# Two attention and feed-forward layers on one core: a new start, and a table that moves single operations in the planner's order

## The chip, the cores and the metric

The kernel runs on one core of one Trainium2 chip. The time is device microseconds of one execution. The engines are named as in the profile: PE multiplies matrices (PEld is its weight load), DVE and ACT work on vectors, POOL is GpSimd, SP issues most of the DMA transfers, and ACT issues some as well.

## What is computed

The input x is 2048 tokens by 640 features in bf16. Two kinds of block alternate, A, B, A, B, with the same weights in both turns:

```python
x = x + _A_ref(_layernorm(x), wq, wk, wv, wo, beta)
x = x + _B_ref(_layernorm(x), w1, w2)
x = x + _A_ref(_layernorm(x), wq, wk, wv, wo, beta)
x = x + _B_ref(_layernorm(x), w1, w2)
```

Block A is attention with 32 heads of 20 features in four segments of 512 tokens. In each segment and head it takes a causal softmax attention within the segment and, with phi(t) = t + 1 for t > 0 and exp(t) otherwise, a read from a memory that the earlier segments wrote:

```python
p = softmax(qs @ ks^T * scale + mask);  a_dot = p @ vs
a_mem = (phi(qs) @ M) / (phi(qs) @ z + 1e-06)
o = sigmoid(beta) * a_mem + (1 - sigmoid(beta)) * a_dot
M = M + phi(ks)^T @ vs;  z = z + sum(phi(ks))
```

The result is multiplied by wo. Block B is max(x @ w1, 0) @ w2 with a hidden width of 1728.

## The kernel before

All weights and x stay on the chip. Work goes by segments of 512 tokens, each four tiles of 128 tokens. For one segment of block A, layer norm is computed token by token on DVE (`stats`: two BN_STATS per tile at L694 and an aggregate at L696), the power -1/2 on POOL (`chain`, L710), the scaling on DVE (L740). The result is transposed by a DMA (`turn`, L716) into `xnT` (for early segments into a part of `hT`). Products with wq, wk (to `stg`) and wv (to `v_aug`) run on PE as groups of five matmuls (`group`, L673). Their results leave PSUM by DVE or ACT (`evac`; L872 and L873 for q and k, L927 for v). q and k go through a scratch tensor in DRAM, and SP loads them back head by head into `pad` (`fill`, L1008), 20 features at the foot of each group of 32 partitions.

Scores (L1192) multiply four heads at a time, in five rounds for each pair of head groups, two rounds' halves together. ACT takes the exponential (L1254, 320 of them), POOL clears what lies behind the diagonal (L1266), and PE multiplies by v (L1286; for the first eight groups, L1325). DMA transposes turn the result back into tokens (`otk`), DVE divides (L1372 to L1380) and adds the memory read (L1072 on PE, L1084 to L1087 on DVE, L1399). The sum `o_sb` is transposed to `oT` (`turn_o`) and multiplied by wo. The memory write is L1129, with its update of `M_sb` and `BD` on DVE. Block B is `ffn` (L1490 and L1491 evict the hidden layer, L1512 adds to x).

A product can be issued in two forms. The full form is one matmul of 128 rows and 128 columns (L673). The quarter form is four matmuls of 128 rows and 32 columns each (L676), which stand on four quarters of the columns; the product with v (L1286) is always of this kind. Scores use 20 rows and 128 columns (the row form).

The order is not written by hand. Each part of the work is a Python generator, a stream, that yields operations; `Sched.run` holds a planned clock for every engine, and at each step takes, of all streams' next operations, the one with the smallest key: planned start plus an allowance, then priority, then segment. The result is a fixed list of instructions for each engine; every engine works its list in order and waits at semaphores. So a planned duration that is changed, or a key that is moved, can change the lists of all engines. PE's form (full or quarter) is chosen by the planner too, from the form that PE last used and from what is due soon.

The start has an order of its own. `loads` issues the transfers for the first four tiles of x (two on SP, two on ACT), then on SP the first columns of wk and wq (c below 2), their remaining columns, wv, and the second segment's x. `warm_pe` multiplies the identity 52 times (L650), which waits for POOL to make it. Tiles 0 and 1 take their statistics on DVE, each with its own POOL chain; tiles 2 and 3 take theirs on ACT (`first_ln_b`): both sums (L805), one mean (L808), both sums of squares (L812), then one chain for both. `first_tile` scales each tile (L752), transposes it on PE (L764) and copies it to `xnT` (L771, L773). `proj_first` then makes q and k for feature chunks c = 0 and 1 in two halves, two tiles (256 tokens) each, and for the other chunks whole. `first_heads` sends chunk 0 and a part of chunk 1 straight from `stg` to the first pads (L988; four transfers on SP, five on ACT). Beta, which every partition needs, is loaded on SP when the second segment's x has been issued (L627), and ACT takes its exponential (L630); the mask `maskg` is made on POOL (L614 to L622).

Of the kernel before, what the change touches and what calls it, by code (L numbers as in the profile page):

```python
# [10 lines left out]
D = 640  # L11
# [161 lines left out]
HOLDERS = 1  # L173
HOLD_TOL = {"pe": 220.0, "act": 150.0, "dve": 200.0, "pool": 0.0, "sp": 0.0}


class Sched:
# [120 lines left out]
    def run(self):  # L298
        while True:
# [24 lines left out]
            for prio, n, st, alts, op, late in heads:  # L324
# [9 lines left out]
                key = (round(start + late), 0.5 if op.urgent else prio, self.rank[id(st[1])], n)  # L334
# [94 lines left out]
def bass_interleave_layers__memory_aug_infini_attn__dense_activation_relu__prompt_kernel(  # L429
    nc, A_x, A_wq, A_wk, A_wv, A_wo, A_beta, B_x, B_w1, B_w2, out,  # L430
):
    with contextlib.ExitStack() as es:
# [13 lines left out]
        ident = sb("ident", [128, 128])  # L446
        warm = sb("warm", [128, 1], dt.float32)
        asum = sb("asum", [128, 4], dt.float32)
        beta_bc = sb("beta_bc", [128, H])
# [3 lines left out]
        stats6 = sb("stats6", [128, 12, 2, 6], dt.float32)  # L453
# [19 lines left out]
        om_sb = sb("om_sb", [128, NJ, D])  # L473
        rden = sb("rden", [128, 2, 2, NJ, 4, 1], dt.float32)
# [48 lines left out]
        def ld(e, name, nbytes, fn, waits=()):  # L523
            tk = yield dma(e, sem_("d_" + name), nbytes, fn, waits, lat=1550.0 if name[:2] == "x0" else 2000.0)
            S.set(name, tks=[tk])
# [7 lines left out]
        def loads():  # L533
# [58 lines left out]
        def consts():  # L592
            tw = yield dve(4, 1, lambda e: e.memset(warm[:], 0.0))
            yield act(4, lambda e: e.activation(warm[:], warm[:], ACT.Exp), [tw], psum=False)
            t0 = yield pool(150, lambda e: e.memset(ident[:], 0.0))
            t1 = yield pool(250, lambda e: e.affine_select(
                out=ident[:], in_=ident[:], compare_op=ALU.not_equal, fill=1.0, base=0,
# [28 lines left out]
            yield Need("x11")  # L626
# [3 lines left out]
            te = yield act(32, lambda e: e.activation(gt[:, 0, :], beta_bc[:], ACT.Exp), [tb], psum=False)  # L630
# [14 lines left out]

        def warm_pe():

            idt = yield Need("ident")
            yield Acq([X])
            tk = yield pe(4600.0, [(lambda e: e.matmul(  # L650
                ps[:, 0, 0:128], ident[:], ident[:], start=True, stop=True), k == 51) for k in range(52)], idt)
            X.release(tk)

# [37 lines left out]
        def stats(t, xt):  # L691
            tk = None
            for c2 in range(2):
                tk = yield dve(320, 1, lambda e, c2=c2: e.bn_stats(  # L694
                    stats6[:, t % 12, c2, :], x_sb[:, t, c2 * 320:(c2 + 1) * 320]), xt)
# [940 lines left out]
```

## Time and profile before

| | |
|---|---|
| time, median of 3 runs | 556.43 us (555.3 to 559.99) |
| span of the profiled execution | 553.7 us; the median lies 2.7 us above it |
| PE busy | 545.7 us (99%), 8,340 matmuls |
| DVE busy | 414.2 us (75%) |
| ACT busy | 408.7 us (74%) |
| POOL busy | 191.9 us (35%) |
| chain that ended last | 89% PE, 5% DVE, 2% DMA, 2% ACT |
| granted clock | 1.000 |

The profile's page is one execution. Its own time is known as its span, from the first to the last instruction; what lies around it in a timed run is taken as the difference to the median. Busy shares are means over the whole span, so the views by stretch and the timeline tell more: the timeline gives start and length in us of runs of equal instructions, with the idle time ahead of them and what ended it in brackets. A run of n equal matmuls is as long as n - 1 distances from start to start and one matmul from its start to its end (0.30 us for 320 elements, 0.38 us for 512), since matmuls overlap.

### The profile page before, as it was taken

The numbers are of one execution on the slowest core, as the hardware profiler recorded it, in microseconds if no ns is written. First come the engines' busy times: TensorE is split into PE (matmuls) and PEld (weight loads), VectorE is DVE, ScalarE is ACT, GpSimd is POOL, SyncE is SP. The second block draws the span as 40 slices with busy tenths as digits, with TensorE's granted clock in tenths as the row PEclk, the third lists the DMA queues.
The fourth block names the chain that finished last, engine by engine and source line by source line (L and its number), as shares of the span: only waits on it lengthen the run. The fifth ranks groups of instructions, "written<-read, shape, count | busy, mean of one in ns | idle before, by whom it ended". The sixth has DMA issues, their size and how long they took to land.

```text
span 553.7 us, 19086 instructions
## 1 busy us (share of the span) xinstructions
PE 545.7 (99%) x8340; PEld 308.3 (56%) x8340; DVE 414.2 (75%) x1059; ACT 408.7 (74%) x518; POOL 191.9 (35%) x302
## 2 busy tenths in 40 slices
PE   8999999999999999999999999999999999999998
PEld 7464554455564555646446555565456654657756
DVE  5967989897898988997687998669886886417202
ACT  5699889889877888687887887778874878651140
POOL 5245344343444334343433443034430433301000
DMA  8595999933854138466276332971439322342201
GB/s 271 134 232 158 227 186 211 239 72 45 191 112 91 32 58 199 79 93 92 60 188 107 60 69 21 207 147 22 67 48 223 92 36 54 69 81 28 74 2 51
DMA packets 130292, 61.32 MB, mean 111 GB/s; under 512 B 109090, under 2 KB 120098, under 8 KB 130210
## 3 DMA queue, kind: packets, MB, share of 16 engines
q1 hardware_dynamic: 129648, 59.58, 50.8%
q8 instruction: 65, 1.06, 0.8%
q10 hardware_dynamic: 562, 0.53, 0.3%
q14 instruction: 17, 0.14, 0.1%
HBM read 20.57 MB, written 12.85 MB: 60 GB/s over the span
## 4 chain that ended last, share of the span: by engine, by line
PE 89%; DVE 5%; DMA 2%; ACT 2%; POOL 0%; SPq 0%; issue 0%; ACTq 0%; POOLq 0%
PE ps L673 42%; PE ps L676 27%; PE ps L1192 8%; PE ps L1286 6%; ACT PT L1254 2%; PE ps L1325 1%; PE ps L1072 1%; PE ps L650 1%; DMA oT<-o_sb 1%; DMA otk<-otu 1%; PE ps L1466 1%; PE ps L1129 1%; DVE hT L1490 1%; DVE xn_tok L740 1%; DMA beta_bc<-in_A_beta_dram 1%; DVE o_sb L1380 1%
## 5 line engine op out<-in xcount | busy, mean ns | idle before, releaser
L1254 ACT ACTIVATE PT<-ps 128x1024 bf16<-128x1024 f32 x320 | 309.0, 1026 | 58.6 <-PE ps L1192 57.3
L1266 POOL TENSOR_SCALAR_AFFINE_SELECT PT<-PT 128x512 bf16<-128x512 bf16 x256 | 166.6, 669 | 266.8 <-ACT PT L1254 266.7
L673 PE MATMUL ps<-w_r,hT 128*128 128x320 bf16 x488 | 78.5, 300 | 0.0
L1512 DVE TENSOR_TENSOR x_sb<-x_sb,ps 128x320 bf16<-128x320 bf16 (+1 forms) x65 | 31.1, 479 | 48.1 <-PE ps L676 34.1
L676 PE MATMUL ps<-xnT,w_r 128*32 128x512 bf16 x1092 | 64.8, 379 | 0.1
L1192 PE MATMUL ps<-pad 20*128 20x512 bf16 (+3 forms) x1024 | 63.4, 301 | 1.2 <-ACT PT L1254 1.0
L673 PE MATMUL ps<-xnT,w_r 128*128 128x512 bf16 x247 | 60.9, 380 | 0.0
L673 PEld LDWEIGHTS ps<-w_r,hT 128*128 128x128 bf16 x488 | 45.6, 98 | 23.5 <-issue 6.4
L694 DVE BATCH_NORM_STATS2 stats<-x_sb 128x6 f32<-128x320 bf16 x124 | 56.0, 474 | 2.6 <-DMA x_sb<-in_A_x_dram 2.2
L676 PE MATMUL ps<-w_r,hT 128*32 128x320 bf16 (+1 forms) x1428 | 52.4, 294 | 0.0
L1192 PEld LDWEIGHTS ps<-pad 20*128 20x128 bf16 x1024 | 17.8, 92 | 52.2 <-ACT PT L1254 28.1
L1491 ACT ACTIVATE hT<-ps 128x512 bf16<-128x512 f32 x51 | 30.5, 598 | 20.5 <-PE ps L676 19.6
L676 PEld LDWEIGHTS ps<-w_r,hT 128*32 128x32 bf16 x1428 | 37.0, 97 | 10.2
L676 PEld LDWEIGHTS ps<-xnT,w_r 128*32 128x32 bf16 x1092 | 28.3, 97 | 24.6 <-issue 0.5
L1296 DVE CAST otu<-ps 128x512 bf16<-128x512 f32 x50 | 34.2, 684 | 8.7 <-PE ps L1286 8.2
L1490 DVE TENSOR_SCALAR hT<-ps 128x512 bf16<-128x512 f32 x53 | 36.1, 682 | 6.1 <-PE ps L673 4.6
L1408 DVE TENSOR_TENSOR x_sb<-x_sb,ps 128x320 bf16<-128x320 bf16 x64 | 29.6, 477 | 14.7 <-PE ps L676 7.3
L1286 PE MATMUL ps<-PT,v_aug 128*21 128x128 bf16 (+3 forms) x896 | 40.4, 301 | 0.0
L1037 ACT ACTIVATE stg<-stg 128x512 bf16<-128x512 bf16 x50 | 31.6, 635 | 8.5 <-DVE rtmp L1035 8.5
L673 PE MATMUL ps<-wo_r,oT 128*128 128x320 bf16 x234 | 37.0, 300 | 0.3 <-DMA oT<-o_sb 0.3
L710 POOL TENSOR_TENSOR rstd<-lnU,mhalf 128x2 f32<-128x2 f32 (+2 forms) x26 | 20.3, 780 | 47.5 <-DVE lnU L706 37.6
L673 PEld LDWEIGHTS ps<-xnT,w_r 128*128 128x128 bf16 x247 | 22.2, 97 | 25.3 <-issue 3.7
(109 smaller groups left out, 737.2 us busy)
## 6 DMA issues: line engine op xcount, KB each, us to landing
pad<-scr SPq DMA_DIRECT2D x124, 80.0 KB
scr<-stg SPq DMA_DIRECT2D x34, 256.0 KB, 2.9
out_dram<-x_sb SPq DMA_DIRECT2D x15, 160.0 KB, 2.2
w_r<-in_B_w_dram SPq DMA_DIRECT2D x10, 216.0 KB, 2.5
w_r<-in_B_w_dram SPq DMA_DIRECT2D x13, 160.0 KB, 3.0
x_sb<-in_A_x_dram SPq DMA_DIRECT2D x10, 160.0 KB, 3.4
scr<-w_r SPq DMA_DIRECT2D x5, 256.0 KB, 2.9
wv_r<-in_A_wv_dram SPq DMA_DIRECT2D x1, 800.0 KB, 8.8
```

The costliest lines, as they stand in the source:

```text
L673: return e.matmul(view(dst.ap, b), a, b, start=(k == 0), stop=(k == last))
L676: return e.matmul(view(dst.ap[rows], b), part, b, start=(k == 0), stop=(k == last))
L694: tk = yield dve(320, 1, lambda e, c2=c2: e.bn_stats(stats6[:, t % 12, c2, :], x_sb[:, t, c2 * 320:(c2 + 1) * 320]), xt)
L1037: te = yield act(512, lambda e, q=q: e.activation(q, q, ACT.Exp), [tr] + p, psum=False)
L1192: fns.append([(lambda e, z=z, j=j, hh=hh, N=N, o=o, sl=sl, q=hh % 2: e.matmul(slot.ap[:, q, o:o + N], sl.ap[32 * hh:32 * hh + DH, z, 0, 12 ...
L1254: tx = yield act(1024, lambda e, dst=dst, src=src: e.activation(dst, src, ACT.Exp, scale=SCALE), sc + pw)
L1266: tm = yield pool(600.0, lambda e, reg=reg: e.affine_select(out=reg, in_=reg, pattern=[[0, 4], [1, 128]], compare_op=ALU.is_ge, fill=0.0, ...
L1286: fns.append((lambda e, OD, j=j, hh=hh: e.matmul(OD.ap[32 * hh:32 * hh + DH + 1, 128 * j:L], VAUG[vx(a, s)][:, j, 4 * g + hh, :], pt.ap[:, ...
L1296: te = yield evac(L, 1, lambda e: e.tensor_copy(dst, OD.ap), lambda e: e.activation(dst, OD.ap, ACT.Copy), [tk] + OTU[0].tks)
L1490: th = yield evac(512, 1, lambda e: e.tensor_scalar(hT[:, dc, :], bk.ap[:, :], 0.0, None, ALU.max), lambda e: e.activation(hT[:, dc, :], b ...
L1491: lambda e: e.activation(hT[:, dc, :], bk.ap[:, :], ACT.Relu), [tk] + HT.tks)
L1512: ta = yield dve(n, 1, lambda e: e.tensor_tensor(x_sb[:, t, c0:c0 + n], x_sb[:, t, c0:c0 + n], bk.ap[:, 0:n], ALU.add), [tk], urgent=True)
```

## The change

- A table `SHIFT` is added to the key of the planner, by stream and segment: 86 entries from -3000 to 4300 ns. It moves where an operation is put, and adds none.
- Planned costs change: a pair of score rounds 233 instead of 221 ns, the power on POOL 520 or 700 instead of 740, the first x loads 1470 instead of 1550, and two DVE operations (`BD` and the last of `divide`) are planned with the port that they share with POOL.
- `warm_pe` uses a tile of ones, set by DVE, in the first PT buffer instead of the identity, and 41 matmuls instead of 52; five more stand behind tile 0's transposes. The identity lies in a part of `om_sb`. The first statistics tile has a place for each of the 16 tiles.
- Beta is loaded as one row of 64 bytes, third in ACT's queue, into a tile that is otherwise zero, and a matmul with the ones spreads it to all partitions; ACT's exponential reads it from PSUM.
- `first_ln_b` does sum, mean and sum of squares for tile 2 and then the same for tile 3, each with its own POOL chain, whose first step moves from DVE to POOL. The mask on POOL waits until tile 3 is scaled.
- `proj_first` makes q and k of chunks 0 and 1 in three pieces: tile 0, tile 1, tiles 2 and 3.

```diff
@@ run @@
-                key = (round(start + late), 0.5 if op.urgent else prio, self.rank[id(st[1])], n)
+                key = (round(start + late + SHIFT.get((n, self.rank[id(st[1])]), 0)), 0.5 if op.urgent else prio, self.rank[id(st[1])], n)
@@ loads @@
+            tz = yield Need("beta0")
+            yield from ld("act", "beta", 64, lambda e: e.dma_start(
+                beta_z[0:1, :], bass.AP(tensor=A_beta.tensor, offset=A_beta.offset, ap=[[H, 1], [1, H]])), tz)
@@ consts @@
-            t3 = yield pool(700, lambda e: e.memset(maskg[:], 1.0))
+            ntk = yield Need("normed", 3)
+            t3 = yield pool(700, lambda e: e.memset(maskg[:], 1.0), ntk)
...
-            tb = yield dma("sp", sem_("d_beta"), 16384, lambda e: e.dma_start(
-                beta_bc[:], bass.AP(tensor=A_beta.tensor, offset=A_beta.offset, ap=[[0, 128], [1, H]])))
-            yield Need("stg", 0, 0, 0, 1)
-            te = yield act(32, lambda e: e.activation(gt[:, 0, :], beta_bc[:], ACT.Exp), [tb], psum=False)
+            tb = yield Need("betab")
+            bk, tb = tb[0], tb[1:]
+            te = yield act(32, lambda e: e.activation(gt[:, 0, :], bk.ap[:, 0:H], ACT.Exp), tb)
@@ warm_pe @@
-            idt = yield Need("ident")
+            tw = yield dve(128, 1, lambda e: e.memset(warm_w, 1.0))
+            tz = yield dve(32, 1, lambda e: e.memset(beta_z[:], 0.0))
             yield Acq([X])
-            tk = yield pe(4600.0, [(lambda e: e.matmul(
-                ps[:, 0, 0:128], ident[:], ident[:], start=True, stop=True), k == 51) for k in range(52)], idt)
+            tk = yield pe(107.0 * 41, [(warm_mm, k == 40) for k in range(41)], [tw])
             X.release(tk)
+            tb = yield Need("beta")
+            yield Need("first", 1)
+            bk, tk = yield pe(40.0, [(lambda e, bk: e.matmul(
+                bk.ap[:, 0:H], warm_w, beta_z[:], start=True, stop=True), True)], tb, acq=MISC)
@@ first_tile @@
+            if t == 0:
+                yield pe(380.0, [(warm_mm, False) for _ in range(5)])
@@ first_ln_b @@
-            tch = yield from chain(2, 2, ts, sq=asum[:, 2:4])
+                tk = yield act(D + 130, lambda e, t=t, j=j: e.activation(
+                    j, x_sb[:, t, :], ACT.Copy, accum_out=asum[:, t - 2:t - 1]), w, psum=False)
+                tm = yield act(100, lambda e, t=t: e.activation(
+                    mv[:, t, 0:1], asum[:, t - 2:t - 1], ACT.Copy, scale=1.0 / D), [tk], psum=False)
+                tk = yield act(D + 250, lambda e, t=t, j=j: e.activation(
+                    j, x_sb[:, t, :], ACT.Square, scale=-1.0, bias=mv[:, t, 0:1],
+                    accum_out=asum[:, t:t + 1]), [tm], psum=False)
+                yield Spawn(5, second(t, tk))
...
+        def second(t, tk):
+            tch = yield from chain(t, 1, [tk], sq=asum[:, t:t + 1])
@@ proj_first @@
-            order = [(c, n, h) for h in range(2) for c in range(2) for n in range(2)]
+            order = [(c, n, h) for h in range(len(PIECES)) for c in range(2) for n in range(2)]
```

with `PIECES = ((0, 1), (1, 2), (2, 4))`.

More of the change, by code (lines that the diff above doesn't have):

```diff
@@ L473, in bass_interleave_layers__memory_aug_infini_attn__dense_activation_relu__prompt_kernel @@
         om_sb = sb("om_sb", [128, NJ, D])
+        ident = om_sb[:, 0, 0:128]
         rden = sb("rden", [128, 2, 2, NJ, 4, 1], dt.float32)
@@ L594, in consts @@
             yield act(4, lambda e: e.activation(warm[:], warm[:], ACT.Exp), [tw], psum=False)
-            t0 = yield pool(150, lambda e: e.memset(ident[:], 0.0))
+            t0 = yield pool(150, lambda e: e.memset(ident, 0.0))
             t1 = yield pool(250, lambda e: e.affine_select(
-                out=ident[:], in_=ident[:], compare_op=ALU.not_equal, fill=1.0, base=0,
+                out=ident, in_=ident, compare_op=ALU.not_equal, fill=1.0, base=0,
                 pattern=[[-1, 128]], channel_multiplier=1), [t0])
@@ L702, in chain @@
             sl = slice(t0, t0 + n)
-            if n == 1:
+            if n == 1 and sq is None:
                 tk = yield pool(150, lambda e: e.tensor_scalar(lnU[:, sl], mv[:, sl, 1], 1.0, LN_EPS, ALU.mult, ALU.add), tk)
@@ L859, in proj_part @@
             w = yield Need(nm)
-            for p in ((0, 1) if h is None else (h,)):
-                t = yield Need("xt", a, s, p)
+            i0, i1 = (0, NJ) if h is None else PIECES[h]
+            if h is None or i1 - i0 == 2:
+                for p in range(i0 // 2, i1 // 2):
+                    t = yield Need("xt", a, s, p)
+                    w = w + t
+            else:
+                t = yield Need("turned0", i0)
                 w = w + t
```

64 lines of the change are left out of this document (32 added, 32 removed), and 12 rows, old and new, of the table SHIFT.

## Prediction

> **What bounds the kernel now.** First the page's part 2, the busy share of each engine in 40 slices of 13.8 us:
>
> ```profile
> PE   8999999999999999999999999999999999999998
> DVE  5967989897898988997687998669886886417202
> ACT  5699889889877888687887887778874878651140
> DMA  8595999933854138466276332971439322342201
> ```
>
> PE is full from the second slice on, so the time is PE's work plus the few places in which it stands. Next the table of busy time by stretch, for those places (columns: stretch, its length, then busy time and count of PE, PEld, DVE, ACT, POOL, granted clock, DMA share, GB/s):
>
> ```profile
> 20.00:40.00 20.00, 19.34 (x227) 10.34 (x225) 15.99 (x43) 19.13 (x24) 9.38 (x14) 1.00 0.92 222
> 40.00:60.00 20.00, 18.54 (x308) 9.72 (x308) 16.17 (x44) 19.99 (x23) 11.70 (x18) 1.00 0.67 173
> 240.00:260.00 20.00, 19.51 (x236) 10.18 (x237) 17.20 (x40) 15.80 (x20) 7.39 (x12) 1.00 0.77 120
> ```
>
> From 20 to 60 us ACT is the bound (39.1 of 40 us busy) and PE stands for 2.1 us. PE also stands 0.5 us in 240 to 260, and hardly elsewhere: 59.4 of 60 us are busy from 80 to 140, 240 of 240 from 260 to 500. Then the timeline of the start, for what sets ACT's first exp, and the DMA issues for the weights (last column: us from issue to landing):
>
> ```profile
> 1.59 5.61 PE L650 MATMUL ps<-ident 128*128 128x128 bf16 x52 [1.59 <-POOL mhalf L600]
> 4.36 2.23 SPq L528 DMA_DIRECT2D wv_r<-in_A_wv_dram  x1
> 8.46 0.72 PE L673 MATMUL ps<-xnT,wk_r 128*128 128x256 bf16 x5 [0.70 <-DVE xnT L771]
> 13.92 0.84 PE L673 MATMUL ps<-wv_r,xnT 128*128 128x320 bf16 x5
> 18.25 0.40 PE L1192 MATMUL ps<-pad 20*128 20x512 bf16 x4
> 19.57 0.23 ACT L630 ACTIVATE gt<-beta_bc 128x32 f32<-128x32 bf16 x1 [1.31 <-DMA beta_bc<-in_A_beta_dram]
> 19.71 1.92 ACT L1254 ACTIVATE PT<-ps 128x1024 bf16<-128x1024 f32 x2
> ...
> wv_r<-in_A_wv_dram SPq DMA_DIRECT2D x1, 800.0 KB, 8.8
> ```
>
> The first scores are done near 18.7, but the exp stands behind L630, which waits for beta until 19.57. Since ACT is full from there to 60 us, an earlier first exp moves that whole stage.
>
> **The change part by part.**
>
> *Start, to the first v product (13.92 now).* The warm-up falls from 52 to 41 matmuls, 0.107 us each (5.61/52), and no longer waits for POOL (1.59): it follows a DVE memset behind 0.87 and ends at about 1.15 + 4.4 = 5.5. Tile 0's norm ends at 5.66, tile 1's at 6.84. In the new order of DVE both norms stand ahead of both copies (0.45 each), so tile 0 is copied at 7.3 and the first k piece runs at 7.4; its wk columns are there (issued 1.72, 5.1 us to landing: 6.8). The q piece waits for wq: issued 2.20, 5.7 us, 7.9. Four pieces of 5 x 0.056 us (the pitch of the 128-wide transposes, L764) end at 8.9. Tile 2's sums on ACT no longer wait for tile 3's: 3.55 + 0.93 + 0.20 + 1.02 = 5.7; on POOL 0.25 + 0.57 behind tile 1's, 7.2. Tile 3's follow on ACT to 7.9 and POOL to 8.8; DVE's norm, with an eviction ahead of it, is done at 9.65, transposes and copy at 10.6, and four 256-wide pieces (0.545 each) end at 12.8. Next in PE's order is the first v product, whose weights land at 4.36 + 8.8 = 13.2. So 1.1 us of earlier work becomes 0.67 gained and 0.4 of waiting for DMA. Two short POOL operations (0.25) replace one of DVE (0.16), and the mask on POOL starts behind tile 3's norm, 9.65 instead of 9.21; its 4.7 us end before its first reader, L641 at 20.95. Beta's load leaves SP (0.48 at 16.72). The identity inside om_sb, the longer statistics tile, the port flags and the changed planner costs add no instruction and act through the order alone. Twelve pieces instead of eight cost PE nothing (40 x 0.056 + 20 x 0.109 against 40 x 0.109), and ACT and DVE four more short evictions that lie under these waits.
>
> *First exp.* From the first v product to the first scores PE's order holds 20 matmuls of 0.136 and 7 of 0.216, 4.2 us: scores at 17.5. Their q and k go through SP's four copies, 3.24 us now from 13.44; behind chunk 0's evictions they start at about 12.1, end at 15.4 and land 1.4 us later, 16.9, in time. Beta now is a 64-byte load at the head of ACT's queue, spread by one small matmul right behind the warm-up; nearest rows, the 160 KB loads of that queue, land 2.9 us after issue, so 5.1, before 5.5. L630's wait is gone: first exp 18.0 instead of 19.71, **1.7 us earlier**. Up to the twentieth round of scores ACT's new order holds one eviction and one phi exp more and two v evictions fewer (0.60 + 0.635 - 2 x 0.44 = 0.35 us). The stage ends 1.35 us earlier.
>
> *PE's order behind it.* The new table and planner constants reorder every engine. Counted in the order of both programs, 543 full matmuls become quarters (8,340 instructions become 9,969). Rows for the price:
>
> ```profile
> 250.99 1.26 PE L676 MATMUL ps<-wv_r,xnT 128*32 128x320 bf16 x32
> 252.29 0.58 PE L676 MATMUL ps<-wv_r,xnT 128*32 128x320 bf16 x12
> 252.81 0.40 PE L1192 MATMUL ps<-pad 20*128 20x256 bf16 x8
> 253.14 0.85 PE L673 MATMUL ps<-wv_r,xnT 128*128 128x320 bf16 x5
> 254.33 0.85 PE L673 MATMUL ps<-wo_r,oT 128*128 128x320 bf16 x5 [0.34 <-DMA oT<-o_sb]
> ...
> 128.72 0.97 PE L1129 MATMUL ps<-v_aug,phk 128*128 128x147 bf16 x12
> 129.53 0.30 PE L673 MATMUL ps<-wv_r,xnT 128*128 128x320 bf16 x1
> ...
> 84.77 0.65 PE L1129 MATMUL ps<-v_aug,phk 128*32 128x147 bf16 x48
> 85.24 0.62 PE L676 MATMUL ps<-hT,wk_r 128*32 128x512 bf16 x8
> ```
>
> One matmul lasts 0.30, so 32 quarters are (1.26 - 0.30)/7 = 0.137 a four, and five full ones (0.85 - 0.30)/4 = 0.137: quarters are free. A switch between full, quarter and row form is not: 12 quarters (0.41) from 252.29 let the scores start at 252.81, 0.11 late. Changes of form fall from 336 to 326: **-1.0**. The memory write L1129 takes 0.81 us full (128.72 to 129.53) and 0.47 in quarters, and two long ones and a part of a short one change over: **-0.75**. Of these 1.75, with what was only moved across the twentieth round, 1.0 lies behind that round, where it counts; ahead of it ACT decides. The Trainium skill, "TensorEngine Tiling (Array Packing)", under Restrictions, says that column tiling disables fast weight load, which speaks against 543 more quarters. The rows above show no such price, so by the trace this adds nothing; the page gives no figure that could be added.
>
> *Stall at 248 to 254.* PE stands 0.24 and 0.50 us there: oT, sent by DVE's last sums at 249.1, lands at 254.3. By the means of their rows, DVE's instructions ahead of what PE awaits come to 8.0 us more than PE's own work up to there in the old order and to 0.7 less in the new. **-0.75.** The other later stalls (some 3.5 us in bits) I leave as they are, bounds 0 and twice that.
>
> *Sum*: -1.35 - 1.0 - 0.75 = -3.1, from a span of 553.7 to 550.6. The median of the runs, 556.43, lies 2.7 above the span; carrying that: **553.3 us**.
>
> **The rivals.**
>
> *More stalls go* (0.20). The table moves single operations by 0.1 to 4.3 us, and the bits of later stall may go as well: up to -3.5 more, 549.8. For it: the same planner left only 7 us in 550. Against: at the fifth to nineteenth round ACT's work ahead of PE is 2 to 4 us larger than before.
>
> *The clock comes late* (0.14), the case on the slower side. Now the pitch of the warm-up changes from 0.107 to 0.056 only at 6.9, 5.3 us after its first matmul. Forty-one end after 4.4 us; five more and the transposes, with gaps, must carry it. If PE is still at half speed at the first product (7.4), transposes, 40 pieces of 0.056 and 20 of 0.109 double: up to 5 us, some 1.5 of it in waits that exist anyway, so +3.5 on the first exp and 556.8. It decides from the first product on. The Trainium skill, "TensorE: Matmul & The Clock Gate", Part 1, puts the change near 4 us (within 0.5) of sustained work; by that 4.4 suffice and this rival is nothing. The trace's 5.3 disagrees, and bounds it.
>
> *DMAs become the bound at 52 to 65 us* (0.22). SP issues in order. The second segment's transposed activations, its pads and the k transposes stand behind ACT's operations, with slack against PE cut from 4.4, 8.1 and 14.8 us of work to 0.1, 1.3 and 2.8. PE is later against its own work there, which is why I expect them in time; but a transpose takes 4.0 us to land, and three such waits of 2 to 4 us make 559 to 565.
>
> *The start does nothing* (part of the forecast's own spread): if beta or the pads come no earlier, 1.7 is lost and it is 555.0. If the weights landed earlier than 13.2, 0.4 more is won.
>
> **How the numbers follow.** Forecast case 0.44 (551 to 555.5). About 1%, 5.6 us, is what a measurement of this kernel can tell from no change. Faster than 550.9: the first rival and the forecast's edge, 0.22. Slower than 562: half of the DMA case and what I have not seen, 0.18. Within: 0.60. The range 549.5 to 561 leaves out most of 0.05 below and 0.14 above.
>
> **What would show it.** First v product at 13.2 to 13.3 and waiting for DMA; first exp at 18.0; ACT full to about 58 and 1.4 us ahead at the twentieth round; no PE idle by oT near 250; PE busy in 260 to 500 as now. Wrong: half-speed pitch after 7.4, PE waiting for xn, pad or phk between 52 and 65, or PE below 59 of 60 us in 80 to 140.

## The result, and the profile after

The changed kernel takes 554.17 us (median of 20 runs, 553.01 to 557.88) against 556.14 us for the kernel before in the same session (20 runs). The ratio is 0.9965, with a 95% interval of 0.9954 to 0.9976: 2.0 us less, where 3.1 were forecast. The profiled execution has a span of 552.1 us (553.7 before) and took 554.18 us, so it stands for the median. The gain is real and inside the 1% that was called "within".

The page's part 2 of the changed kernel, busy shares in 40 slices of 13.8 us:

```profile
PE   8999999999999999999999999999999999999998
DVE  4977899899798949987788759987968788745102
ACT  6699779889878878788888858888887779423140
DMA  8596989623861533953377841359138521433101
```

PE is full as before. Busy time by stretch of the changed kernel (stretch, its length, busy time and count of PE, PEld, DVE, ACT, POOL, granted clock, DMA share, GB/s):

```profile
20.00:40.00 20.00, 19.60 (x249) 10.81 (x248) 17.20 (x45) 18.97 (x25) 9.32 (x14) 1.00 0.86 221
40.00:60.00 20.00, 18.57 (x292) 9.31 (x288) 15.40 (x44) 19.95 (x23) 11.83 (x18) 1.00 0.72 188
60.00:80.00 20.00, 19.26 (x181) 11.32 (x180) 17.04 (x50) 13.89 (x21) 5.99 (x9) 1.00 0.89 193
80.00:140.00 60.00, 60.00 (x850) 30.06 (x846) 54.28 (x128) 54.33 (x68) 24.15 (x38) 1.00 0.60 142
240.00:260.00 20.00, 20.00 (x476) 11.23 (x472) 14.68 (x32) 18.05 (x24) 8.48 (x12) 1.00 0.50 90
```

The same view of the kernel before, for the two stretches that the prediction did not show:

```profile
60.00:80.00 20.00, 20.00 (x225) 11.97 (x227) 17.24 (x53) 16.03 (x24) 6.62 (x10) 1.00 0.95 215
80.00:140.00 60.00, 59.39 (x872) 29.16 (x868) 52.97 (x129) 54.73 (x71) 24.58 (x36) 1.00 0.67 143
```

The stall near 250 us is gone (PE busy 20.00 of 20, 19.51 before), and so are the bits at 80 to 140. But PE now stands 0.74 us at 60 to 80, where it stood for nothing before. Idle PE behind 57 us comes to 0.91 us after 1.10 before.

The start, from the timeline and the DMA issues of the changed kernel:

```profile
1.12 4.56 PE L666 MATMUL ps<-PT 128*128 128x128 bf16 x41 [1.12 <-DVE warm L610]
8.90 0.45 PE L702 MATMUL ps<-xnT,wq_r 128*128 128x128 bf16 x5 [1.12 <-DMA wq_r<-in_A_wq_dram]
14.21 0.84 PE L702 MATMUL ps<-wv_r,xnT 128*128 128x320 bf16 x5
18.70 0.40 PE L1230 MATMUL ps<-pad 20*128 20x512 bf16 x4
15.42 0.19 ACT L646 ACTIVATE gt<-ps 128x32 f32<-128x32 f32 x1
19.13 1.02 ACT L1292 ACTIVATE PT<-ps 128x1024 bf16<-128x1024 f32 x1 [2.49 <-PE ps L1230]
...
wv_r<-in_A_wv_dram SPq DMA_DIRECT2D x1, 800.0 KB, 9.7
```

Beta's exponential (L646) is done long before the first exp, as forecast, and the exp no longer waits for it. But the first columns of wq landed at 8.85 instead of the 7.93 that the trace of before shows, and wv at 14.1 instead of 13.2. PE stood 1.12 us for wq, and the 1.7 us expected at the first exp came out as 0.58.

The longest links of the chain that ended last, of the changed kernel (start, us, what), confirm the place:

```profile
2.20 6.66 DMA wq_r<-in_A_wq_dram
...
36.51 4.79 DMA pad<-scr
41.89 18.42 ACT PT L1292 x20
```

The chain of before began with the warm-up and went through beta's load; now it begins with wq. A second transfer, a pad's, ends at 41.3 inside the stage in which ACT is the bound.

Three marks split the span: the first exp, the 37th (in the last rounds of the ACT stage) and the start of the last matmul.

| trace | first exp | 37th exp | last matmul | 37th exp to last matmul |
|---|---|---|---|---|
| before | 19.71 | 56.77 | 551.09 | 494.32 |
| after | 19.13 | 56.34 | 549.53 | 493.19 |

So of 1.56 us, 0.43 come from the stage up to the twentieth round and 1.13 from behind it.

### The profile page after: what moved, and what is told of

It reads as the page before. It is cut to its first block, busy times and chain, and to the rows that moved or that the text cites. A ratio compares the mean times of both kernels' runs of the same rounds, so it can differ in the third digit from the quotient of the medians.

```text
span 552.1 us, 22367 instructions
## 1 busy us (share of the span) xinstructions
PE 544.5 (99%) x9969; PEld 311.6 (56%) x9969; DVE 417.5 (76%) x1052; ACT 413.0 (75%) x531; POOL 195.8 (35%) x305
## 4 chain that ended last, share of the span: by engine, by line
PE 88%; ACT 6%; DMA 2%; DVE 2%; SPq 1%; issue 0%
PE ps L705 43%; PE ps L702 27%; PE ps L1230 9%; PE ps L1324 6%; ACT PT L1292 5%; PE ps L1110 2%; DMA wq_r<-in_A_wq_dram 1%; PE ps L1504 1%; DMA pad<-scr 1%; PE ps L1167 1%; DMA pad<-stg 0%; ACT stg L1075 0%; SPq L1026 0%; DVE stats L723 0%; DVE o_sb L1418 0%
## 5 line engine op out<-in xcount | busy, mean ns | idle before, releaser
L705 PE MATMUL ps<-xnT,w_r 128*32 128x512 bf16 x1464 | 89.1, 380 | 0.0
L705 PE MATMUL ps<-w_r,hT 128*32 128x320 bf16 (+1 forms) x1868 | 71.2, 295 | 0.0
L702 PE MATMUL ps<-w_r,hT 128*128 128x320 bf16 x378 | 62.4, 300 | 0.0
L705 PEld LDWEIGHTS ps<-xnT,w_r 128*32 128x32 bf16 x1464 | 36.0, 97 | 33.6 <-issue 4.4
L705 PEld LDWEIGHTS ps<-w_r,hT 128*32 128x32 bf16 x1868 | 47.5, 97 | 12.7 <-issue 0.2
L702 PEld LDWEIGHTS ps<-w_r,hT 128*128 128x128 bf16 x378 | 34.8, 98 | 18.2 <-issue 5.3
L910 DVE CAST stg<-ps 128x512 bf16<-128x512 f32 (+1 forms) x41 | 27.3, 668 | 16.6 <-PE ps L705 9.5
L702 PE MATMUL ps<-xnT,w_r 128*128 128x512 bf16 x154 | 37.4, 380 | 0.0
L705 PE MATMUL ps<-wo_r,oT 128*32 128x320 bf16 x864 | 36.7, 300 | 0.0
L1334 DVE CAST otu<-ps 128x512 bf16<-128x512 f32 x45 | 30.7, 682 | 5.5 <-PE ps L1324 4.2
```

Source lines behind the costliest of these rows:

```text
L702: return e.matmul(view(dst.ap, b), a, b, start=(k == 0), stop=(k == last))
L705: return e.matmul(view(dst.ap[rows], b), part, b, start=(k == 0), stop=(k == last))
L1334: te = yield evac(L, 1, lambda e: e.tensor_copy(dst, OD.ap), lambda e: e.activation(dst, OD.ap, ACT.Copy), [tk] + OTU[0].tks)
```

## Experiments

From the third run on, most kernels follow a written list: the order and forms of one of the two kernels, operation by operation, so that an edit does not shift the planner's choice. Their line numbers are 20 higher (L722 is L702). The code for it, the same in all of them:

```diff
@@ run @@
+            if self.follow.on:
+                told = self.follow.next(heads)
+                if told is not None:
+                    (_, _, st, _, op, _), (end, start, k, _), mode = told
...
-                op.mode = self._mode(op)
+                op.mode = mode if mode is not None else self._mode(op)
```

### What holds the start

**The changed kernel again**, no edit.

> The changed kernel as it is, for a second trace of its start. In its first trace wk, wq and wv landed at 7.1, 8.9 and 14.1 us (6.8, 7.9 and 13.2 before) and the fourth tile of x at 6.3 instead of 4.6. If chance made these landings late, this trace shows them elsewhere, by some tenths of a us or more, and near the old ones in about half of such traces. If the change makes them late (beta's load, or ACT's loads issued at 1.15 instead of 0.97), wq lands again at 8.7 to 9.0 and wv at 13.9 to 14.2. Time 0.35% under the kernel before in either case.

Measured: 555.6 us (10 runs), ratio 0.9984 (0.9959 to 1.0009). In its profile wq landed late again (8.81, and wv at 13.99), as if the change fixed these landings; a third set, below, has 8.04 and 13.29. Then something else came on top. Busy time by stretch:

```profile
6.00:8.00 2.00, 1.13 (x18) 0.82 (x16) 1.38 (x4) 1.12 (x4) 1.17 (x3) 1.00 1.11 333
8.00:9.00 1.00, 0.42 (x7) 0.25 (x5) 0.60 (x2) 0.83 (x2) 0.08 (x1) 0.89 1.10 330
9.00:10.00 1.00, 1.00 (x11) 1.00 (x10) 0.22 (x1) 0.28 (x1) 0.66 (x2) 0.50 1.09 335
10.00:12.00 2.00, 2.00 (x21) 1.97 (x19) 0.49 (x2) 1.26 (x3) 1.57 (x4) 0.50 1.06 363
12.00:14.00 2.00, 1.97 (x26) 1.64 (x24) 0.56 (x3) 0.92 (x4) 1.79 (x6) 0.95 0.82 277
```

The last three columns are granted clock, DMA share and GB/s. PE was busy for only 1.89 of the 3.41 us from 5.36 to 8.77, in pieces of work with gaps of at most 0.6 us; then the clock was 0.50 for 3.4 us (0.22 + 1 + 2 + 0.20 of the last four stretches). The pieces of q and k ran at half speed, and the first v product began at 15.35 although wv had landed at 13.99. The first exp came at 20.27.

**Beta's load left out.** Beta stays zero, so its gates are those of zero.

```diff
@@ loads @@
-            yield from ld("act", "beta", 64, lambda e: e.dma_start(
-                beta_z[0:1, :], bass.AP(tensor=A_beta.tensor, offset=A_beta.offset, ap=[[H, 1], [1, H]])), tz)
+            yield Op([("act", 500.0, [], 0.0)], tz)
+            S.set("beta", tks=tz)
```

> The changed kernel in the same order on every engine, but beta is not loaded (it is taken as zero, so this part of the computation is left out). Theory that the 64-byte load in ACT's queue holds the weights up: wq lands at 7.9 and wv at 13.2, the q piece of tile 0 starts at 8.0 instead of 8.9, the first exp comes at about 18.2 instead of 19.1, and the span falls by 0.8 to 0.9 us. Rival that ACT's two loads of x, issued 0.18 us later than before, get mixed with wk's: nothing changes, wq at 8.9. Rival chance: anything between.

Measured: 554.4 us (10 runs), ratio 0.9974 (0.9954 to 0.9994). Its timeline shows the start that the prediction had worked out:

```profile
7.95 0.45 PE L722 MATMUL ps<-xnT,wq_r 128*128 128x128 bf16 x5
13.28 0.84 PE L722 MATMUL ps<-wv_r,xnT 128*128 128x320 bf16 x5
18.03 1.02 ACT L1312 ACTIVATE PT<-ps 128x1024 bf16<-128x1024 f32 x1 [2.03 <-PE ps L1250]
```

The first exp stands at 18.03 (forecast 18.0), and the 37th is 1.33 us earlier than before (forecast 1.35). So the working of the start holds where the weights land when they did in the trace of before. That beta's load makes them late does not follow: in the kernels below that load it, wq landed anywhere from 7.23 to 8.99, and the median without the load is no lower than the changed kernel's.

**ACT's loads first**: in the list, ACT issues its two tiles of x before it loads its function table.

```diff
@@ list for ACT @@
+x_sb<-in_A_x_dram x2
 LoadActFuncSet
 warm<-warm
-x_sb<-in_A_x_dram x2
 beta_z<-in_A_beta_dram
```

> The changed kernel in the same order, but ACT issues its two loads of x before the small exponential that waits for DVE, so at 0.80 instead of 1.15. Theory that the late issue mixes them with wk's load: the fourth tile of x lands at 4.5 instead of 6.3, wq at 7.9 and wv at 13.2, the first exp at about 18.2, the span 0.8 to 0.9 us shorter. Theory that beta's load is the cause: the landings of wq and wv stay at 8.9 and 14.1, tile 3 of x lands somewhat earlier, and the time stays within 0.2 us.

Measured: 555.2 us (10 runs), ratio 0.9986 (0.9965 to 1.0006). wq landed at 7.39 and wv at 12.70, yet the first v product ran at 13.75. The timeline names the new holder:

```profile
6.36 0.45 PE L814 MATMUL ps<-om_sb,xn_tok 128*128 128x128 bf16 x5 [0.79 <-DVE xn_tok L801]
```

Tile 0 of x landed at 3.73 instead of 3.1, with two more tiles issued at the same time, and its transposes set the start. In this trace, moving one transfer up pushed another. It need not: the kernel without its table, below, also issues these tiles at 0.80, and there tile 0 landed at 3.46 and the first exp came at 18.08.

### What a form costs

**Every quarter product that may be full made full**, order unchanged: 412 changes of form instead of 326, all 86 of them behind the twentieth round.

```diff
@@ list, each product that has both forms @@
-t31 120 0 cols
+t31 120 0 full
...
```

> The changed kernel in the same order on every engine, with every product in full form (the products with v stay in quarters). Changes of form rise from 326 to 412, and nine memory writes go back to full form: 4 x 0.35 + 5 x 0.22 = 2.5 us. If a change of form costs 0.1 us and quarters are free in themselves: 86 x 0.1 + 2.5 = 11 us slower than the changed kernel, a little less where PE stands anyway (10 to 11). If quarters cost PE something (more instructions, no fast weight load), less than that, and below 2.5 if the change of form were free.

Measured: 566.94 us (4 runs), ratio 1.0198 (1.0181 to 1.0216). Part 1 of the two pages, the changed kernel first:

```profile
PE 544.5 (99%) x9969; PEld 311.6 (56%) x9969; DVE 417.5 (76%) x1052; ACT 413.0 (75%) x531; POOL 195.8 (35%) x305
```

```profile
PE 555.8 (98%) x5241; PEld 297.7 (53%) x5241; DVE 417.9 (74%) x1052; ACT 413.7 (73%) x531; POOL 194.4 (34%) x305
```

Half as many instructions do the same products and PE is busy 11.3 us longer. From the 37th exp to the last matmul it is 503.84 against 493.19 us, 10.65 us more. Not all of it is changes of form: nine memory writes went back to the full form, which is longer for them, because in quarters most of their matmuls run over 42 or 63 columns (the `128x42` and `128x63` of the rows) instead of 147 or 168. One of them, in the changed kernel and in this run (0.47 and 0.81 us to the next product):

```profile
86.41 0.65 PE L1167 MATMUL ps<-v_aug,phk 128*32 128x147 bf16 x48
86.88 1.27 PE L705 MATMUL ps<-hT,wq_r 128*32 128x512 bf16 x20
...
88.67 0.97 PE L1187 MATMUL ps<-v_aug,phk 128*128 128x147 bf16 x12
89.48 1.24 PE L722 MATMUL ps<-hT,wq_r 128*128 128x512 bf16 x5
```

With the 2.5 us that the expectation reckons for the nine (2.6 by their rows), some 8.1 us are left for 86 changes: 0.095 us each. (The rest of the difference in time is a wait of 1.61 us at 39 us, and the half clock behind it.) Both halves of the forecast's price stand: quarters are free (0.137 us a four against 0.137 in full, in the prediction's rows), and a change of form costs 0.1. The Trainium skill, "TensorEngine Tiling (Array Packing)", Key Properties, says that a change of tiling mode drains TensorE, without a figure; this trace agrees that a change costs time, 0.095 us.

### Start and order apart

Four kernels put parts of the two orders together, and one leaves out the table.

**New start, old order**: the changed kernel up to the first v product, then the order of before.

```diff
@@ Sched, changed kernel @@
+        self.follow = Follow('t31')   # t31: the stream of the v products; list: the order of before
```

> The changed kernel's start up to the first v product, and from there the operations in the order and the forms of the kernel before (336 changes of form, 2,123 full matmuls of attention x V as before). It tells the start's worth alone. Theory (start and order add): the start is worth between 0.4 us (what the trace of the changed kernel showed on the 36th exp) and 1.35 us (what the run without beta's load showed), and the order's 1.0 to 1.6 is gone: 555.3 (554.8 to 555.9). Rival 1 (the start is all of it): 554.2 to 554.6. Rival 2 (the start does nothing by the end, later waits take it back): 556.1 to 556.5.

Measured: 556.18 us (12 runs), ratio 1.0009 (0.9991 to 1.0027), so no gain. Its 37th exp is 0.39 us earlier than before's, and this lead lasts to 91 us. There the timeline has a wait for which the profile names no cause:

```profile
91.52 0.62 PE L725 MATMUL ps<-xnT,w_r 128*32 128x512 bf16 x8 [0.53 <-issue]
```

From the 37th exp to the last matmul it is 494.84 us; less that 0.53 it is 494.31, the figure of before. Whether the other executions wait there too isn't known.

**Old start, new order**: the kernel before up to the first v product, then the changed order.

```diff
@@ Sched, kernel before @@
+        self.follow = Follow('t31')   # list: the order of the changed kernel
```

> The start of the kernel before up to the first v product, and from there the operations in the changed kernel's order and forms (326 changes of form). It tells the order's worth alone. Theory (start and order add): the ten changes of form and the memory write as quarters are worth 1.0 to 1.1, the stalls left out near 250 us 0.75, less what new stalls at 60 to 66 us took: 554.9 (554.2 to 555.6). Rival 1 (the order is worth nothing without the start, because it was made for the earlier first exp): 556.0 to 557. Rival 2 (the order is all of it): 553.9 to 554.4.

Measured: 559.55 us (10 runs), ratio 1.0053 (1.0036 to 1.007). None of the three had expected this. The first exp comes at 22.63, 2.9 us later than before:

```profile
20.86 0.60 PE L693 MATMUL ps<-xnT,wq_r 128*128 128x512 bf16 x2 [2.59 <-ACT w_r L947]
...
22.79 1.06 PE L693 MATMUL ps<-xnT,wq_r 128*128 128x512 bf16 x2
```

A q product stands in PE's queue until ACT has evicted a v product (L947). ACT was held up in its own queue, where beta's exponential now stands ahead of that eviction:

```profile
18.97 0.23 ACT L650 ACTIVATE gt<-beta_bc 128x32 f32<-128x32 bf16 x1 [3.34 <-DMA beta_bc<-in_A_beta_dram]
20.36 0.44 ACT L947 ACTIVATE w_r<-ps 128x320 bf16<-128x320 f32 x1 [1.17 <-issue]
```

The old start loads beta late, and the new order asks for it early. Two q matmuls of 512 columns then last 1.06 instead of 0.59: the clock is at half from 22 to 25.4 us, again behind a thin stretch. The new order is made for the new start's times and doesn't carry over to the old one.

**Late order alone** (before up to the 40th exp, then the changed order) and **early order alone** (the mirror image).

```diff
@@ lists @@
+late order:  before up to the 40th exp  + after from there (326 changes of form)
+early order: after up to the 40th exp   + before from there (336 changes of form)
```

> The kernel before, its start and its order up to the 40th exp (about 60 us), and from there the changed kernel's order and forms (326 changes of form). It takes the changed kernel's order without the first 60 us, where the run of the old start with the whole new order lost 3.7 us. Theory (what the change gains is the order behind the 20th round: ten changes of form, the memory write as quarters and the stall near 250 us, less the new waits at 60 to 66): the last product 1.1 to 1.3 earlier than the kernel before's, 554.9 (554.4 to 555.4). Rival 1 (the order behind 60 us is only good with a lead from the start): within 0.5 of the kernel before. Rival 2 (the whole of it, the start's share included, comes from here): 554.2 or less.

> The mirror image: the changed kernel up to the 40th exp, from there the order and forms of the kernel before. Theory (the first 60 us are worth the 0.4 us that the profiles of the changed kernel show on the 36th exp, and nothing behind it): 555.7 (555.3 to 556.2); with the new start and the old order the time was 556.2 against 556.1 before. Rival 1 (the lead is lost in the first waits behind the 20th round, as the old order's w_r and oT waits end no earlier): 556.0 to 556.6. Rival 2 (the start carries the change): 554.6 or less.

Measured: 557.35 us, ratio 1.002 (1.0003 to 1.0037), and 558.9 us, ratio 1.0043 (1.0017 to 1.0068), 12 runs each. Both are slower than before, and the waits say why. First the late order, at its seam:

```profile
63.21 1.21 PE L1345 MATMUL ps<-w_r,PT 128*128 128x21 bf16 x40 [2.14 <-ACT v_aug L947]
```

then the early order:

```profile
39.78 1.25 PE L722 MATMUL ps<-hT,wk_r 128*128 128x512 bf16 x5 [1.54 <-DVE M_sb L1202]
```

The seam of the late order costs 2.14 us, and half clock for 3.4 us behind it. In the early order PE waits 1.54 us for the memory update that follows its first memory write; the changed kernel has the same instructions up to there and no such wait. DVE's rows tell why:

```profile
38.45 0.72 DVE L1093 TENSOR_SCALAR rtmp<-stg 128x512 bf16<-128x512 bf16 x1 [2.14 <-DMA scr<-stg]
39.10 0.62 DVE L1202 COPY M_sb<-ps 128x462 f32<-128x462 f32 x1
```

An operation ahead of the update in DVE's queue waited for a transfer to the scratch tensor, which took 4.2 us to land (34.24 to 38.43) where it took 2.6 in the changed kernel's profile (33.02 to 35.58). In the run with all products full the same transfer took 4.7, with a wait of 1.61 us on PE. So this wait comes from a landing, in the part that the early order shares with the changed kernel, and not from the cut. The cut cost as well: from the 37th exp to the last matmul it is 497.63 us against 494.32 before, 1.76 of the difference more idle PE (0.85 in one wait at 110 us) and 1.55 more work.

**The table left out**: `SHIFT` empty, all else as in the changed kernel, the planner's own order.

```diff
-SHIFT = {
-    (5, 0): -3000, (7, 0): -700, (7, 1): 400, (7, 2): -1000, (7, 4): 4300, (7, 5): -1100, (7, 6): -2700,
...
+SHIFT = {}
```

> The changed kernel with the table of moved operations empty: the same start, and the planner's own order behind it (334 changes of form, 2,052 full matmuls of attention x V). Theory (the table pays by its eight changes of form, 0.8 us, and by the stall near 250 us, 0.75 us): 555.4 (554.8 to 556.2), and the trace shows TensorE idle again near 250 us. Rival 1 (the table moves waits about and gains nothing): 554.0 to 554.6. Rival 2 (without the table the planner's order runs into longer waits): 557 or more.

Measured: 570.77 us (6 runs), ratio 1.0262 (1.0226 to 1.0299). The planner's order behind the new start runs into waits of 0.2 to 2.2 us that add up to 13.4, most of it at 20 to 40, 60 to 80, 100 to 160 and 289 us. The first large one, and busy time by stretch from there:

```profile
34.93 0.61 PE L1217 MATMUL ps<-pad 20*128 20x512 bf16 x4 [2.15 <-DMA pad<-scr]
```

```profile
30.00:36.00 6.00, 3.26 (x37) 1.48 (x34) 2.43 (x7) 3.39 (x5) 2.04 (x3) 0.85 0.90 248
36.00:40.00 4.00, 4.00 (x55) 1.94 (x54) 1.33 (x3) 2.88 (x4) 0.63 (x1) 0.50 0.74 162
40.00:46.00 6.00, 6.00 (x36) 2.25 (x37) 2.18 (x7) 4.40 (x5) 2.44 (x4) 0.63 0.36 90
```

PE is busy 3.26 of 6 us, and the clock is at half for 10.2 us from 34.2 on (1.8 + 4 + 4.4 of the three stretches). In all six executions the mean granted clock was below 1.0. The 86 entries are worth some 16 us to this start: they keep PE's queue from running into results that are not there yet (one pad's transfer, and mostly ACT's exponentials and DVE's evictions), and the clock up.

### The clock

**More warm-up between the waits**: 9 matmuls more behind tile 0's transposes and 14 behind tile 1's.

```diff
@@ first_tile @@
+            if t == 1:
+                fns = fns + [(lambda e, bk: warm_mm(e), False) for _ in range(14)]
...
-                yield pe(380.0, [(warm_mm, False) for _ in range(5)])
+                yield pe(380.0, [(warm_mm, False) for _ in range(14)])
```

> The changed kernel in its own order, with 23 more of the warm-up's 128x128 matmuls between tile 0's transposes, tile 1's transposes and the first k piece (9 behind tile 0's transposes, 14 behind tile 1's), so that TensorE stands idle less between 5.5 and 8.9 us. In the repeat of the changed kernel TensorE was busy only about half of the stretch from 5.5 to 8.9 us (waits of 0.16, 0.45, 0.42 and 0.58 us), and from 8.9 to 12.1 the granted clock was 0.50; four of its ten executions had a mean clock of 0.997, where half of 3.2 us is 0.003 of the span, and these took 555 to 558.7 us against 553 to 555.8. Theory (a thin stretch at the start halves the clock for one stretch of about 3.3 us in some executions): with the gaps filled, no execution or one in ten has a mean clock below 1.0, the slow tail above 555.5 us goes, and the median is 554.0 (553.5 to 554.6). Rival 1 (the halving comes from outside or from later stretches): the share of executions below 1.0 stays at two or three in ten, and the time is the changed kernel's 554.2 to 555.6. Rival 2 (the added matmuls themselves are in the way): the first v product starts 0.3 to 0.8 us later than wv's landing and the time rises to 554.8 to 555.5 with the clock at 1.0.

Measured: 555.05 us (12 runs), ratio 0.9978 (0.9963 to 0.9992). PE was busy 3.21 of the 3.4 us from 5.5 to 8.9. One of 12 executions had a mean clock below 1.0, against 11 of 42 of the changed kernel over three sessions (and 11 of 96 of the kernel before): fewer, but too few runs to tell it from chance. The time is no better, and the profile, with the v product 0.13 us behind wv's landing, does not show why.

**Less warm-up**: 21 matmuls instead of 41, and one instead of five behind tile 0's transposes.

```diff
@@ warm_pe @@
-            tk = yield pe(107.0 * 41, [(warm_mm, k == 40) for k in range(41)], [tw])
+            tk = yield pe(107.0 * 41, [(warm_mm, k == 20) for k in range(21)], [tw])
@@ first_tile @@
-                yield pe(380.0, [(warm_mm, False) for _ in range(5)])
+                yield pe(380.0, [(warm_mm, False) for _ in range(1)])
```

> The changed kernel in its own order with 21 warm-up matmuls instead of 41, and one instead of five behind tile 0's transposes, so that TensorE stands idle from about 3.4 to 5.7 us and has done 2.2 us of work instead of 4.4 before the first transposes. It forces the case that the forecast priced as the clock coming late, and tests whether thin work in a stretch is what lowers the clock (with 23 matmuls more, one of 12 executions had a mean clock below 1.0; in the changed kernel it was 3 of 20, 4 of 10 and 4 of 12). Theory (the clock follows how busy TensorE was in the stretch before; the pieces then run at half speed): most executions show matmuls of 128 columns at 0.107 us between 7.4 and 10 us, the mean clock is 0.997 or less where the record has it, the first exp comes 1.5 to 3.5 us later than 18.2 to 19.1, and the time is 1.5 to 3.5 above the changed kernel: 556 to 558. Rival 1 (the start waits for transfers anyway, so half speed hides in those waits): first exp within 0.7 and 554.2 to 555.3. Rival 2 (the clock comes up after a fixed time whatever TensorE does): the pitch is 0.056 from about 7 us on as before, with the time unchanged.

Measured: 556.28 us (11 runs), ratio 1.0 (0.9979 to 1.0022): the whole gain is gone. Its timeline:

```profile
7.72 0.69 PE L722 MATMUL ps<-xnT,wk_r 128*128 128x128 bf16 x5
8.76 0.72 PE L722 MATMUL ps<-xnT,wq_r 128*128 128x128 bf16 x5 [0.34 <-DMA wq_r<-in_A_wq_dram]
9.26 0.74 PE L722 MATMUL ps<-xnT,wk_r 128*128 128x128 bf16 x5
9.80 0.74 PE L722 MATMUL ps<-xnT,wq_r 128*128 128x128 bf16 x5
...
20.72 1.02 ACT L1312 ACTIVATE PT<-ps 128x1024 bf16<-128x1024 f32 x1 [2.48 <-PE ps L1250]
```

From one group of five to the next it is 0.54 us (9.26 to 9.80), 0.107 a matmul; in the changed kernel it is 0.28 (9.19 to 9.47), 0.056. It stays so until about 13.6. The first v product began at 15.80, 1.9 behind wv's landing, and the first exp 1.6 us later than in the changed kernel, with wq landing at much the same time (8.71 and 8.85). The theory's 1.5 to 3.5 and 556 to 558 hold; that the waits for transfers hide it doesn't.

### The changed kernel a third time

The changed kernel from its own list, no other edit.

> The changed kernel once more, on the chip of the two runs above, since two sets of runs gave it 2.0 and 0.7 us under the kernel before. Theory (the part behind 60 us and the part ahead of it add): its gain is the sum of the gains of the two runs above within 0.5 us, 1.4 to 2.0, and one to three executions in ten have a mean granted clock of 0.997. Rival (the two parts need each other, the late order the early lead): its gain is larger than the sum by over 0.6.

Measured: 554.56 us (12 runs), ratio 0.9968 (0.9945 to 0.9991). Since both halves alone were slower than before, their gains don't add to this one, and the rival holds in its wording. But what the halves lost, they lost in waits that the profile of the whole order does not have, and one of these came from a late landing, so they don't say what each part contributes in the whole. The marks do:

| trace | wq landed | first exp | 37th exp | 37th exp to last matmul |
|---|---|---|---|---|
| after | 8.85 | 19.13 | 56.34 | 493.19 |
| again | 8.81 | 20.27 | 58.77 | 493.40 |
| third | 8.04 | 18.18 | 55.83 | 493.29 |
| beta's load left out | 7.90 | 18.03 | 55.44 | 493.02 |
| ACT's loads first | 7.39 | 18.68 | 55.99 | 493.58 |
| more warm-up | 8.18 | 18.31 | 56.24 | 493.08 |
| less warm-up | 8.71 | 20.72 | 57.90 | 493.98 |
| before | 7.93 | 19.71 | 56.77 | 494.32 |
| new start, old order (less the 0.53) | 8.02 | 18.83 | 56.38 | 494.31 |

The last column hardly knows the start: 493.0 to 494.0 with the new order, 494.3 with the old. The 37th exp varies by 3.3 us with the start alone.

## Why the prediction was right, and where not

The direction, the case (within 1%) and the range came out; the size was 3.1 against 2.0, and 1.6 in the two spans. Both parts fell short, and nothing cancelled: 0.43 instead of 1.35 up to the twentieth round, and 1.13 instead of 1.75 behind it. The 2.7 us carried from span to median was no fixed term: in the later sessions a timed run of the kernel before lies 1.7 to 1.9 us above its own span and one of the changed kernel 2.0 to 2.2, so the rest was a profiled execution quicker than the median. By the steps:

- **Start to the first v product (13.25 forecast).** 14.21 in the profiled execution. The warm-up, the order of the pieces and the evictions ran as worked out; what failed is "wq: issued 2.20, 5.7 us, 7.9" and "4.36 + 8.8 = 13.2". The landings were taken from one execution, as if the kernel fixed them. In eight traces with the change's own loads in their order, the first wq columns landed from 7.23 to 8.99 and wv from 12.48 to 14.18; two of them, from one chip, have 7.23 and 8.81, so it isn't the chip alone.
- **First exp (18.0).** 19.13. It was 18.03 to 18.31 in five of the traces with wq at 8.2 or earlier (18.68 with tile 0 late, 18.83 with the old order behind the start), and 19.06 to 19.13 with wq at 8.85 to 8.99 and the clock up. Beta's part, the end of L630's wait, was right.
- **ACT stage (-1.35).** -0.43 in the profiled execution, -0.94 in the third set, -1.33 without beta's load. Besides the landings, "an earlier first exp moves that whole stage" did not hold everywhere. It did without beta's load, where 1.68 us at the first exp became 1.33. From the 17th to the 21st exp the lead fell by 0.34 us in the profiled execution and by 0.65 in the third set; in the first, the chain shows the pad's transfer that lands at 41.3, and in the run "again" PE waits 1.34 us for a pad at 43.9. So a lead is lost where a transfer comes no earlier; what took it in the third set was not followed up.
- **Changes of form and the memory write (-1.0 where it counts).** Behind the 37th exp the gain was 1.13, 0.92 and 1.03 in the three profiles of the changed kernel. Idle PE behind 57 us was 1.10 before, and 0.91 and 1.17 in the first and third of these, so the work itself fell by 0.9 to 1.1. This step is right, and its price per change (0.1) is what the run with all products full leaves beside its memory writes, 0.095.
- **Stall at 248 to 254 (-0.75).** Right in its place: 0.49 of idle PE there is now 0.00, and no product waits for oT. The size was mixed: the product that waits for oT starts 0.50 late (the profile counts 0.34 of it as idle), while the 0.24 stands ahead of the memory write at 248.93, which does not read oT. But "the other later stalls I leave as they are" failed, for new waits took it back. From the timeline of the changed kernel:

```profile
60.45 0.84 PE L702 MATMUL ps<-wv_r,hT 128*128 128x320 bf16 x5 [0.24 <-ACT PT L1292]
65.94 0.68 PE L1167 MATMUL ps<-w_r,phk 128*128 128x147 bf16 x8 [0.47 <-DVE mv L725]
```

  The second is the memory write, waiting for phi(k). In the run "again" the profile names its transfer for the same wait (0.93 us), in the old start with the new order too (1.09), so the DVE named here had probably been done.
- **Rivals.** *More stalls go*: no; they moved. There was also less to win than the 3.5 us counted: by busy time PE stood 2.7 us behind 20 us, oT's wait left out, and 2.1 of them where ACT is the bound. *DMAs become the bound at 52 to 65 us*: the wait for phk is the place it meant, at 0.5 to 1.1 us instead of three of 2 to 4. *The clock comes late*: not as priced in the profiled execution, where the distance between matmuls halved (full clock) at 6.93 and stayed. That was only 0.4 us ahead of the first product, and partly luck: the 5.3 us from the first matmul to full clock, which the prediction took from one trace, is a sample too. In twelve traces with the whole warm-up it was 2.9 to 5.8 us. So it is no empty case. Forced, it cost 1.6 to 2.5 us on the first exp (against the first and the third set) instead of the 3.5 forecast, and the whole gain. In another form, half clock behind a thin stretch, it is the cause of the start's 20.27 in the run "again". The mean granted clock was below 1.0 in 11 of the 42 executions of the changed kernel; their median was 556.9 us and that of the others 553.9. Where in the span the clock fell in the executions without a trace is not known.

What stays open is whether the landings vary by chance alone or by something in the start. One landing does move with the change: the fourth tile of x came at 5.0 to 7.0 us in the nine traces where ACT issues its first load at 1.15, and at 4.6 to 5.4 in the five where it does so at 0.80 or 0.97; for wq the ranges are 7.2 to 9.0 and 7.4 to 8.3. Open too is how the start's and the early order's worth divide, since no cut between the orders was free of its own waits, and why the transfer to the scratch tensor took 2.5 to 2.8 us to land in six traces of this order and 4.0 to 4.7 in three others (1.54 us of PE's time at 39 us in the early order, 1.61 with all products full, 0.29 with more warm-up).

## What to carry to other kernels

A landing read from one execution is a sample: with the same start, these weights landed over a range of 1.8 us, and a forecast that hangs on one should carry that spread as a term. An order that a planner made for one set of times is one piece: half of it with another start, or the start without its table, lost 1 to 15 us against the kernel before, mostly at one or two places where an in-order queue stands, and then again through the clock. Where TensorE is full, count changes of form rather than instructions.

## What the runs showed of the hardware

- A stretch of 3.41 us in which TensorE was busy for 1.89 us, with no gap over 0.6 us, was followed by half clock for 3.41 us (the run "again"); so were stretches with 1.74 (all products full), 1.27 (late order) and 1.16 (old start, new order). With 2.29 of 3.41 us busy, from 6.93 on in the changed kernel's profile, it was not. But in the early order 1.76 (37.34 to 40.75, a stretch of the same steps) was not followed by half clock either, so the busy share alone does not decide. The Trainium skill, "TensorE: Matmul & The Clock Gate", Part 1, gives a window of 3.4 us, which agrees with the length; the rule of its section on HAM oscillation, that gaps above about 3.4 us are to be avoided, does not cover this trace, where no gap was over 0.6 us.
- Each of these falls came a whole number of 3.41 us behind the first change to full clock: one in the run "again" (5.36 and 8.77), five in the old start with the new order (4.95 and 22.02), ten with all products full (4.83 and 38.96), seventeen in the late order (5.64 and 63.66). The first change itself came at 4.1 to 7.0 us in the twelve traces with the whole warm-up, which began at 1.1 in the new start and at 1.6 in the old. This suggests that whether a thin stretch costs anything depends on where these steps happen to lie in an execution.
- With less warm-up the matmuls run at half speed (0.107 us apart) until 13.6 us, while the profile's clock column reads 1.00. At the start of a span the column can't be relied on; the distance between matmuls tells.
- A change between the full, quarter and row forms costs 0.1 us of TensorE here, and four quarter matmuls take no longer than one full one (0.137 us at 320 columns): 4,728 instructions fewer, with 86 changes more and nine memory writes in full form, made the work behind the twentieth round 10.7 us longer.
